# Two of 24 one-megabyte token loads are cut into three DMAs each

## The chip, the cores and the metric

The kernel runs on one core of a Trainium2 chip. The metric is the device time of one execution in microseconds (us). Before the change the median of three runs is 199.24 us (199.17 to 199.47).

## The reference: a gated recurrence, then a soft mixture of experts

Inputs are `x` and `f_logit`, both 4 batches x 5056 tokens x 256 channels in float32, a vector `lower_bound` of 256, and the weights `phi` (256 x 32), `w1` (8 x 256 x 1024) and `w2` (8 x 1024 x 256). The first stage is a recurrence over the tokens of each batch:

```
f = lower_bound + (1 - lower_bound) * sigmoid(f_logit)
h[t] = f[t] * h[t-1] + (1 - f[t]) * x[t]          # y[t] = h[t]
```

The second stage takes all 20224 rows of y as one list. `logits = y @ phi` gives 32 slots. A softmax over the rows weighs the rows into 32 slot inputs; each of the 8 experts takes four of them through `relu(slot @ w1) @ w2`; a softmax over the slots then mixes the 32 slot outputs back into every row. The output is 20224 x 256 in float32, 20.7 MB. The softmax over all rows means that no output row can be written before the whole recurrence and the experts are done.

## The kernel before: one ordered stream, then the experts, then the output

**Tiling.** The 5056 tokens of a batch are cut into 10 groups of 512 (the last but one is shorter). A unit `n` is one group of one batch, 40 in all. Units 8 to 31 are "long" ones: a pair of units (`n` even and `n + 1`) is 1024 consecutive tokens of one batch. `load(n)` brings a pair into an `f_t` tile and an `x_t` tile of 128 partitions x 2048 floats; partition p holds eight consecutive tokens, 8 KB that lie in one piece in memory. So a long pair is two DMAs of 1 MB (line 211), and there are 12 such pairs: n = 8, 10, ..., 30. The units before and after them are loaded with smaller DMAs (lines 225, 216 and 220). Each kind of tile has three buffers, so the load of pair n waits until the buffer of pair n - 6 has been read: `f_t` by ScalarE's sigmoid (line 235, `gate`), `x_t` by GpSimd's product (line 246, `enter`).

**The steps of a unit.** `gate`: ScalarE takes the sigmoid of a pair (`s_t`). `enter`: GpSimd multiplies it by x (`u_t`, one per unit). TensorE transposes both to channels (lines 261 and 267, `sp` and `up`). `decay`: ScalarE makes the factors `a` (lines 295, 302). `scan`: VectorE runs the recurrence along the tokens, two instructions per unit (line 313, `h`). TensorE transposes h back (line 326, `hp`), VectorE or ScalarE copies it out (line 343, `ht`); logits, exponentials and the accumulation of the slot inputs follow (lines 357, 366, 407).

**What sets the order.** The program is written out in order by hand (`manual_schedule`): each engine runs its instructions in the order of the loop over `n`, with waits on semaphores. All token loads are issued from the SP queue. `load(n + 6)` is called in iteration n, so the pair n = 20 is issued in iteration 14 and its sigmoid stands in iteration 16. The hardware DMAs issued from SP and ACT take their completion semaphores in turn from eight; a DMA waits for the DMA that used its semaphore before it.

**Weights.** The expert weights are loaded by the GpSimd queue (`load_w`, lines 136 and 146), cast from float32 to bf16 on the way, with the number per iteration in `W_AT`: 8 of w1, then 8 of w2, the last one in three parts. Most are issued after unit 31. The last two of w2 use an `f_t` buffer under the name `w_t`.

**The end.** After the last scan come the slot inputs, the two products of the experts (lines 624, 660, 671; line 671 is `so_ps` for experts 4 to 7, four groups of eight matmuls, the last sixteen of which read `w_t`), `slot_out` (lines 687, 688), and then the output stage: matmuls (708, 758), scaling by VectorE and ScalarE, and stores of up to 2 MB from SP (lines 734, 746, 772, 789). Short filler matmuls (`spin`, line 151, and `idle`, line 183) keep TensorE busy.

Of the kernel before, what the change touches and what calls it, by code (L numbers as in the profile page):

```python
# [18 lines left out]
def kernel(  # L19
# [10 lines left out]
    nc = tc.nc  # L30
# [5 lines left out]
    P = 128  # L36
    DC = D // P
    FC = F // P
    R = 4
    G = P * R  # L40
# [5 lines left out]
    def first(g):  # L46
        return g * G if g < n_grp - 1 else S - G
# [114 lines left out]
    with tc.tile_pool(name="sp2", bufs=3) as sp2, \  # L162
# [24 lines left out]
        def long(n):  # L187
            return 2 * B <= n < n_unit - 2 * B

        def place(n):  # L190
            if long(n):
                t, j = divmod(n, 2 * B)
                return 2 * t + j % 2, j // 2
            return divmod(n, B)
# [4 lines left out]
        def tokens(src, n, k):  # L199
            g, b = divmod(n, B)  # L200
            v = src[ds(b, k), ds(first(g), G)]
            return v.rearrange("b (p r) d -> p b r d", r=R)

        def load(n, k=2):
            for src, dst, tag in ((f_logit, fs, "f_t"), (x, xs, "x_t")):
                if n % 2 == 0:
                    dst[n // 2] = ld.tile([P, 2, R, D], F32, name=tag, tag=tag)
                t = dst[n // 2]
                if long(n):
                    g, b = place(n)  # L210
                    nc.sync.dma_start(
                        out=t.rearrange("p u r d -> p (u r) d"),
                        in_=src[b, ds(first(g), 2 * G)].rearrange("(p r) d -> p r d", r=2 * R))
                elif n // B == odd:
                    b, t0 = n % B, first(odd)
                    nc.sync.dma_start(
                        out=t[:, 0, R3],
                        in_=src[ds(b, 2), ds(t0 + P * R3, L)].rearrange("b t d -> t b d"))
                    for m in range(2):
                        nc.sync.dma_start(  # L220
                            out=t[:, m, ds(0, R3)],
                            in_=src[b + m, ds(t0, P * R3)].rearrange("(p r) d -> p r d", r=R3))
                else:
                    for m in range(n, n + k):
                        nc.sync.dma_start(out=t[:, ds(m % 2, 1)], in_=tokens(src, m, 1))
# [237 lines left out]
        for n in range(SINGLE):  # L463
            load(n, 1)
# [15 lines left out]
        for n in range(n_unit):  # L480
            if n < SINGLE - 2:
# [9 lines left out]
                if n % 2 == 0:  # L491
                    unit(load, n + AHEAD)
                unit(enter, n + 3)
                rep_constants(n)
            else:
                end = n >= n_unit - 6
                if n % 2 == 0:
                    unit(load, n + AHEAD)
                    if n == SINGLE - 2:
                        to_tokens(n - 1)  # L500
                        keep_tokens(n - 1)
                    if not end and n >= SETTLED:
                        unit(gate, n + 4)
                else:
                    unit(decay, n + 1)
                    if n < SETTLED:
                        gate(n + 3)
                    if n == n_unit - 5:
                        gate(n + 3)
                        exps(odd - 1)  # L510
# [37 lines left out]
                elif not end and long(n - 1):  # L548
                    if n % B == 0:
                        g = (n - 1) // (2 * B) * 2  # L550
# [48 lines left out]
    with tc.tile_pool(name="ew", bufs=1) as ew, \  # L599
# [35 lines left out]
        for q in range(E // Q):  # L635
# [4 lines left out]
            if q == 0:  # L640
                nc.tensor.matmul(cs_ps, rep2, cs1, start=True, stop=True)
                src = ht_ps.rearrange("p f (j s) -> p f j s", s=NS)[:, :, :, ds(0, SPE)]
                src = bass.AP(tensor=src.tensor, offset=src.offset,
                              ap=[list(src.ap[0]), [P, FC], [NS + SPE, Q], [1, SPE]])
# [6 lines left out]
            for j in range(Q):  # L651
                s0 = (Q + j) * SPE
                src = ht_ps[:, :, ds(j * NS + s0, SPE)]
# [177 lines left out]
```

## Time and profile before

| | |
|---|---|
| median of three runs | 199.24 us |
| the profiled execution's own time | 198.55 us |
| its span (first to last instruction) | 196.8 us |
| busy share of the span: PE, DVE, ACT, POOL | 77%, 73%, 70%, 52% |
| HBM read and written | 58.23 MB, 20.71 MB |
| 1 MB loads of `f_t`, of `x_t` | 12 and 12; 13.1 and 12.1 us from issue to landing (median) |
| the weights, `w_sb` of 512 KB written | 14 DMAs, 10.9 us from issue to landing (median) |

The profile shows one execution; times in it count from the start of the span. PE is TensorE, DVE VectorE, ACT ScalarE, POOL GpSimd, SP the engine that issues most DMAs. A row of a timeline is: start, duration, engine, line of the kernel, operation, written tile and read tiles, shape, number of instructions, and in brackets how long the engine stood idle before it and what ended that. The page cuts the span into 40 slices of 4.92 us; a digit is the busy share in tenths. A DMA runs on up to 16 DMA engines of the core; the trace keeps every packet with its start and duration, and for each DMA the moment at which each of its engines reported the end. A DMA has landed with the last of these.

### The profile page before, as it was taken

How to read it: one execution, taken by the hardware profiler on the slowest of the kernel's cores; microseconds unless marked ns; L12 is line 12 of the kernel's file. 1: busy time of each engine (PE TensorE's matmuls, PEld its weight loads, DVE VectorE, ACT ScalarE, POOL GpSimd, SP SyncE). 2: the span in 40 equal slices, each digit the busy share in tenths (PEclk: the TensorE clock that was granted, in tenths of full speed). 3: DMA queues.
4: the chain of work that ended last, by engine and by line, in shares of the span. 5: the costliest groups of instructions: out<-in, count | busy, mean ns of one | idle time of the engine just before them, and what ended most of it. 6: DMA issues, size and time to landing. Idle time of an engine off the chain costs nothing.

```text
span 196.8 us, 3233 instructions
## 1 busy us (share of the span) xinstructions
PE 151.1 (77%) x1198; PEld 105.9 (54%) x1198; DVE 143.4 (73%) x164; ACT 138.4 (70%) x195; POOL 103.2 (52%) x78
## 2 busy tenths in 40 slices
PE   0687589789979979997998878999979999950000
PEld 0475458577766857765776666558953533410000
DVE  2669789998899999999999999423278878740000
ACT  3688778899699998999997695622079799980000
POOL 2689586894988588894979967291030000000000
PEclk9999999996999999999999999999995555555555
DMA  5999999999999999999999999999739999999995
GB/s 203 418 423 417 430 430 420 428 426 338 403 425 428 393 343 423 426 413 306 406 422 376 265 221 213 213 213 214 130 136 424 428 444 433 426 430 426 426 426 216
DMA packets 14305, 70.75 MB, mean 360 GB/s; under 512 B 1601, under 2 KB 2882, under 8 KB 10322
## 3 DMA queue, kind: packets, MB, share of 16 engines
q1 hardware_dynamic: 11520, 62.00, 76.0%
q0 software_dynamic: 2624, 8.42, 21.5%
q8 instruction: 9, 0.15, 0.3%
q10 hardware_dynamic: 146, 0.13, 0.2%
q14 instruction: 6, 0.05, 0.1%
HBM read 58.23 MB, written 20.71 MB: 401 GB/s over the span
## 4 chain that ended last, share of the span: by engine, by line
PE 37%; DMA 22%; DVE 20%; issue 4%; POOL 4%; ACT 2%; ACTq 0%; SPq 0%; DVEq 0%; POOLq 0%
DVE h L313 15%; DMA x_t<-in_x_dram 14%; PE op L758 12%; DMA f_t<-in_f_logit_dram 7%; POOL u_t L246 4%; DVE ht L343 4%; PE hp L326 3%; PE up L267 3%; PE op L708 2%; PE so_ps L671 2%; PE sp L261 2%; PE lg L357 2%; PE slot_ps L407 1%; PE tail L151 1%; PE tail L390 1%
## 5 line engine op out<-in xcount | busy, mean ns | idle before, releaser
L246 POOL TENSOR_TENSOR u_t<-s_t,x_t 128x1024 bf16<-128x1024 bf16 (+1 forms) x39 | 82.5, 2127 | 22.4 <-ACT s_t L235 12.0
L313 DVE TENSOR_TENSOR_SCAN h<-a,h,up 128x512 bf16<-128x512 f32 (+1 forms) x72 | 86.9, 1252 | 3.7 <-PE up L267 2.5
L235 ACT ACTIVATE s_t<-f_t 128x2048 bf16<-128x2048 f32 (+2 forms) x23 | 38.4, 1669 | 7.2 <-DMA f_t<-in_f_logit_dram 7.2
L326 PE MATMUL hp<-ident_f,h 128*128 128x128 f32 (+1 forms) x160 | 29.2, 307 | 7.8 <-DVE ht L343 5.9
L326 PEld LDWEIGHTS hp<-ident_f,h 128*128 128x128 f32 (+1 forms) x160 | 23.4, 207 | 17.6 <-DVE ht L343 10.4
L261 PE MATMUL sp<-ident_f,s_t 128*128 128x128 f32 x144 | 21.3, 291 | 6.8 <-ACT s_t L235 4.6
L295 ACT ACTIVATE a<-sp,lbs 128x1024 f32<-128x1024 bf16 x24 | 25.4, 1115 | 0.6 <-PE sp L261 0.6
L758 PE MATMUL op<-slot_bd,etall 64*128 64x512 bf16 x62 | 24.5, 608 | 0.1
L769 ACT ACTIVATE oc<-op,rrow 128x256 f32<-128x256 f32 x60 | 22.7, 488 | 1.5 <-PE op L758 0.9
L763 DVE TENSOR_TENSOR oc<-op,rrow 128x1024 f32<-128x1024 f32 x16 | 19.3, 1222 | 4.7 <-PE op L758 4.5
L261 PEld LDWEIGHTS sp<-ident_f,s_t 128*128 128x128 f32 x144 | 17.3, 150 | 8.8 <-ACT s_t L235 5.1
L302 ACT ACTIVATE a<-sp,lbs 128x512 f32<-128x512 bf16 (+2 forms) x22 | 17.8, 856 | 3.8 <-PE sp L261 3.5
L267 PE MATMUL up<-ident_f,u_t 64*128 64x64 f32 x192 | 17.6, 230 | 2.4 <-POOL u_t L246 2.4
L183 PE MATMUL slot_ps<-rep,ident_f 128*128 128x256 f32 x54 | 17.7, 423 | 1.0 <-POOL rep L86 1.0
L267 PEld LDWEIGHTS up<-ident_f,u_t 64*128 64x128 f32 x192 | 13.9, 138 | 6.3 <-POOL u_t L246 2.8
L758 PEld LDWEIGHTS <-etall 64*128 64x128 bf16 x62 | 9.1, 154 | 14.1 <-issue 11.4
L343 DVE COPY ht<-hp 128x512 f32<-128x512 f32 (+1 forms) x22 | 14.7, 670 | 1.4 <-PE hp L326 1.4
L343 ACT COPY ht<-hp 128x512 f32<-128x512 f32 (+1 forms) x18 | 10.4, 580 | 6.6 <-PE hp L326 6.5
L313 DVE TENSOR_TENSOR_SCAN h<-a,up 128x512 bf16<-128x512 f32 x8 | 9.3, 1208 | 2.5 <-PE up L261 2.5
L183 PEld LDWEIGHTS slot_ps<-rep,ident_f 128*128 128x128 f32 x54 | 8.6, 194 | 3.4 <-issue 1.3
L357 PE MATMUL lg<-h,phi 128*32 128x512 bf16 (+1 forms) x80 | 9.6, 390 | 0.0
L261 PE MATMUL up<-ident_f,u_t 128*128 128x128 f32 x48 | 8.9, 312 | 0.5 <-POOL u_t L246 0.5
(108 smaller groups left out, 146.5 us busy)
## 6 DMA issues: line engine op xcount, KB each, us to landing
f_t<-in_f_logit_dram SPq DMA_DIRECT2D x12, 1024.0 KB, 13.1
x_t<-in_x_dram SPq DMA_DIRECT2D x12, 1024.0 KB, 12.1
out_dram<-oc SPq DMA_DIRECT2D x6, 2048.0 KB, 11.8
w_sb<-in_moe_w_dram POOLq DMA_DIRECT2D x14, 512.0 KB, 10.9
f_t<-in_f_logit_dram SPq DMA_DIRECT2D x12, 512.0 KB, 8.4
x_t<-in_x_dram SPq DMA_DIRECT2D x12, 512.0 KB, 9.9
out_dram<-oc SPq DMA_DIRECT2D x4, 896.0 KB, 5.8
out_dram<-ob SPq DMA_DIRECT2D x1, 2048.0 KB, 9.0
```

The lines of the kernel that those rows point to most:

```text
L183: nc.tensor.matmul(slot_bank[:, 1], ident_f, wide_rep, start=False, stop=False, skip_group_check=True)
L235: nc.scalar.activation(s_t, f_t, ACT.Sigmoid, scale=-1.0)
L246: nc.gpsimd.tensor_tensor(uts[n][:, :r], s_t[:, :r], x_t[:, :r], ALU.mult)
L261: nc.tensor.transpose(ps[:, :, r], t[:, r], ident_f)
L267: nc.tensor.transpose(v[:, :, r], t(r)[k].bitcast(F32), ident_f[k, k])
L295: nc.scalar.activation(a, sp[:, :, :, :, o], ACT.Identity, scale=nomlb[:, ds(o, 1)], bias=1.0)
L313: nc.vector.tensor_tensor_scan(h[:, :T, o], decays[n // 2, o][:, n % 2, :T], up[:, :T, o], hs[number(g - 1, b)][:, ds(used(g - 1) - 1, 1), ...
L326: nc.tensor.transpose(hp[:n_p, r], hw[:, :n_p, r], ident_f)
L343: copy(hts[g][:n_p, b].rearrange("p r d -> p (r d)").bitcast(F32), hps.pop(n)[:n_p].rearrange("p r c -> p (r c)"))
L758: nc.tensor.matmul(op[:, i_r].rearrange("p u d -> p (u d)"), ew[:, :, r + i_r], slot_bd[ds(j * 2 * NS, 2 * NS)].rearrange("s u d -> s (u d)"),
L763: nc.vector.tensor_tensor(ob[:, :, ds(r, k)].rearrange("p u r d -> p r u d"), op[:, ds(0, k)], scale[:, ds(r, k)].unsqueeze(3).broadcast_t ...
L769: nc.scalar.activation(ob[:, u, r + i_r], op[:, i_r, u], ACT.Copy, scale=scale[:, r + i_r, ds(u, 1)])
```

## The change: n = 20 is loaded as 112 + 8 + 8 partitions

For the pair n = 20 each of the two 1 MB loads (`f_t` and `x_t`) becomes three DMAs into the same tile: partitions 0 to 111, 112 to 119 and 120 to 127. The other 22 long loads stay one DMA of 128 partitions. The bytes, their places and the order of the loads are the same; SP issues four DMAs more.

```diff
+        SKEWED = 20
+
         def load(n, k=2):
...
                 if long(n):
                     g, b = place(n)
-                    nc.sync.dma_start(
-                        out=t.rearrange("p u r d -> p (u r) d"),
-                        in_=src[b, ds(first(g), 2 * G)].rearrange("(p r) d -> p r d", r=2 * R))
+                    into = t.rearrange("p u r d -> p (u r) d")
+                    rows_in = src[b, ds(first(g), 2 * G)].rearrange("(p r) d -> p r d", r=2 * R)
+                    shares = (P - 16, 8, 8) if n == SKEWED else (P,)
+                    for i, k in enumerate(shares):
+                        part = ds(sum(shares[:i]), k)
+                        nc.sync.dma_start(out=into[part], in_=rows_in[part])
```

## The prediction

> **What bounds the kernel now.** I read the page's slices first, then the chain of work that ended last, then the rows around the three places where a load can hold the end: the sigmoid of pair 20, the recurrence on VectorE, and the last weights.
>
> ```profile
> DMA   5999999999999999999999999999739999999995
> GB/s 203 418 423 417 430 430 420 428 426 338 403 425 428 393 343 423 426 413 306 406 422 376 265 221 213 213 213 214 130 136 424 428 444 433 426 430 426 426 426 216
> ```
>
> The sixteen DMA engines are full from slice 1 to slice 27 (5 to 138 us) and again in the output stage. The 213 GB/s of slices 23 to 27 is no idleness: the weights are read as float32 and written as bf16, so the engines still read some 426 GB/s. One stream of loads and weights thus runs without a gap until about 142 us.
>
> ```profile
> 39.50 14.40 DMA f_t<-in_f_logit_dram
> 60.78 2.35 DVE h L313 x2
> 140.74 1.88 PE so_ps L671 x16
> 142.64 0.36 DVE slot_out L687
> 155.50 19.24 PE op L758 x48
> ```
>
> The chain goes over loads until 53.90 us (pair 18's `f_t`), then over VectorE and TensorE. At the end of the middle part it stands on the last sixteen products of the experts, then `slot_out`, then the output stage, whose 2 MB stores leave at the full DMA rate (slices 30 to 38) and end the span. So whatever moves `slot_out` moves the end by as much. Those sixteen products against the eight before them:
>
> ```profile
> 137.59 1.03 PE L671 MATMUL so_ps<-w_sb,wide 128*128 128x256 bf16 x8
> 140.57 2.03 PE L671 MATMUL so_ps<-w_t,wide 128*128 128x256 bf16 x16
> 127.62 0.53 POOL L146 DMA_DIRECT2D w_t<-in_moe_w_dram  x1 [1.91 <-DMA w_sb<-in_moe_w_dram]
> DMA to landing us min/median/max: 14.6/17.3/18.5
> 140.00:142.00 2.00, 2.00 (x21) 1.78 (x20) 0.76 (x2) 0.00 (x0) 0.00 (x0) 1.00 0.59 96
> ```
>
> One takes 0.273 us by its own row, and eight take 1.03, so they follow each other at (1.03 - 0.273) / 7 = 0.108 us. Sixteen should take 0.273 + 15 x 0.108 = 1.89 and took 2.03: about 0.13 us of waiting. The last `w_t` part is issued at 127.62 and, with the shortest time to landing of the four, lands at 142.2, where the wait ends. Landing and TensorE are level there: the landing ends last, by 0.13 us.
>
> The last row is the table by stage (PE, PEld, DVE, ACT, POOL, then the granted clock 1.00, the DMA share 0.59 and GB/s). In 140 to 142 us the engines are only 59% busy: some are through long before others. The trace's landing marks say how unequal. Against the earliest engine, the sixteen end the last weight DMA at 0, .14, .20, .38, .52, .85, .86, .91, 1.28, 1.36, 1.42, 1.50, 1.64, 1.66, 1.70 and 1.86 us. For the first loads the spread is 0.4 us. The steps come with the fetches of instructions (queue q8, 16 KB packets) and ACT tables (q14, 8 KB), each served by one engine: the one at 29.4 us sets one engine back 1.4 us behind its fellows, and it stays back, since no engine ever runs out of work to catch up in.
>
> **The change part by part.**
>
> *The split of the bytes.* A 1 MB load is 128 rows of 8 KB, eight to an engine. At 16 engines and 428 GB/s (slices 4 and 5 have 430) a row takes 8192 / 26.75 = 0.306 us on its engine; the packet records have the same step. 112 rows give seven to each engine. The 8-row pieces are the question: no row before shows one. From one side there is `lb_row`, one row. Queue q10 holds it and one output store of 128 rows, 146 packets in all: 128 + 16 completions for the store leave one packet and one completion for it, so one row used one engine. From the other side, a load of 128 rows uses all sixteen. I take eight engines with a row each, nearest to one engine for a row. If both pieces use the same eight, those get 7 + 1 + 1 = 9 rows and the other eight get 7. Over `f_t` and `x_t` that is +2 rows and -2 rows: the first eight end everything later by 2 x 0.306 = 0.61 us, the others earlier by 0.61. The bounds: pieces spread over sixteen shift nothing; a piece on a single engine puts 7 + 16 rows there against 8, 15 more, twice, 30 x 0.306 = 9.2 us.
>
> [...]
>
> *The shift at the end.* The engines are never idle, so a shift at 60 us is still there at 142. The last landing becomes the larger of (latest of the loaded eight + 0.61) and (latest of the others - 0.61). Which of the sixteen the loaded eight are, no view tells. If the engine at 1.86 is among them, +0.61. If the latest among them is the one at 1.70, 1.66 or 1.64, then +0.45, +0.41 or +0.39. Half the chance lies on the first, most of the rest on the next two: I take +0.5. The end waits on this landing already, so the price is paid in full.
>
> *Pair 20 in mid stream.* The same shift reaches the loads: `f_t` of pair 20 by up to 0.31 us, all later ones by up to 0.61.
>
> ```profile
> 58.94 1.91 ACT L235 ACTIVATE s_t<-f_t 128x2048 bf16<-128x2048 f32 x1 [0.24 <-DMA f_t<-in_f_logit_dram]
> 61.68 0.75 PE L326 MATMUL hp<-ident_f,h 128*128 128x128 f32 x4
> 61.78 2.15 POOL L246 TENSOR_TENSOR u_t<-s_t,x_t 128x1024 bf16<-128x1024 bf16 x1 [0.94 <-PE lg L357]
> 63.73 2.45 DVE L313 TENSOR_TENSOR_SCAN h<-a,h,up 128x512 bf16<-128x512 f32 x2
> 70.28 5.01 DVE L313 TENSOR_TENSOR_SCAN h<-a,h,up 128x512 bf16<-128x512 f32 x4
> ```
>
> ScalarE's sigmoid waits for this load. Behind it on ScalarE stand the copy `ht` (60.76, ends 61.33) and the decays, and TensorE's `hp` at 61.68 waits for `ht`: 0.3 us late is just covered by the 0.35 between. GpSimd's product starts at 61.78, and x lands by the marks at 61.25; 0.61 late is 61.86, 0.1 us lost. The scan that needs these products starts at 70.28, 2 us after its transposes. VectorE is the bound here and its row shows next to no idle time; from pair 24 on, the `f_t` and `x_t` waits of ScalarE and GpSimd (0.5 to 0.6 us each) grow by 0.6 under about 1 us of room before the next scan. Zero, with at most 0.3 us on the way to a place where the landing of the weights is late by more.
>
> *Four more DMAs on SP.* Each issue takes 0.33 us, and two follow the first at 47.16 and at 51.56. The eight semaphores now come round sooner: the `f_t` of pair 22, issued at 51.98, must wait for pair 18's (landed 53.90), 1.9 us later; that of pair 24 (56.31) for pair 20's first piece, about 2.5 us later. Behind them SP has only more loads. By the landing marks their data start at about 59.6 and 64.6 us, when the queue gets to them, so 5 us or more remain. Cost 0 as long as the queue holds over 2 MB; without that cover 2 us.
>
> *Fixed cost of a small DMA.* In the packet records one load follows another on an engine with a completion packet of some 6 ns between: four more on eight engines, 0.02 us. The other bound is the small token DMAs of line 216 (128 KB), which by the marks end 0.3 to 1.0 us before the next: at most 4 us if a 64 KB piece cost that alone. I take 0.02, the row of the same queue in the same state. [...]
>
> *Sum.* 0.5 + 0 + 0 + 0.02 = +0.5 us on the profiled execution's 198.55 (span 196.8 and 1.75 around it), 199.05. That execution is 0.69 below the median of the runs; on 199.24 the forecast is 199.75 us. What a measurement of this kernel can tell from no change is about 0.2%, 0.40 us.
>
> **The rivals.**
>
> *A, the forecast: a late engine gets the extra rows.* For it: eight engines lie at 1.28 or later, and it takes only one of the four latest among the loaded eight. 199.6 to 199.9. Chance 0.64.
>
> *B, not slower: the late ones are all relieved.* If the four latest are all among the relieved eight and no loaded engine was beyond 1.25 us, the last weight lands earlier. For it: exactly eight engines lie beyond 1.25, as if they were one half. If so, the landing moves to the larger of 1.86 - 0.61 and .91 + 0.61, 0.34 us earlier, but TensorE then ends last, and only the 0.13 us of waiting is gained: 199.1. More could come only through the waits on loads in mid stream, which VectorE covers. Chance 0.20, of which 0.07 beyond the measurement.
>
> *C, no shift:* the pieces go over all sixteen, or each over a different eight. 199.24. Against it: `lb_row`. Chance 0.10.
>
> *D, the pieces are dear:* one engine takes a whole piece, or each pays on its own. 203 to 208. Chance 0.06.
>
> **How the numbers follow.** Of A four fifths lie beyond 0.40 us (the cases at 0.61, 0.45 and 0.41): 0.51; D adds 0.06, C's scatter 0.01: slower 0.58. Faster is B's 0.07 and 0.02 of C's scatter: 0.09. The same: 0.33. The range takes A with 0.1 us of scatter, and B and C below: 199.0 to 200.0; it leaves out D and B's larger gain. A's own range is 199.6 to 199.9.
>
> **What would show it.** In the profile after: pair 20's pieces with 8 completions each; engines of the last `w_t` DMA ending up to 0.6 us later against TensorE's sixteen products, which then take 2.4 to 2.6 us in place of 2.03; `slot_out` at about 143.1; VectorE's scans as before. If `w_t` lands by 142.0 and the sixteen take 1.9, B holds. The forecast fails if a gap in the engines' work lets the late ones catch up, or if the fetches fall on other engines in other executions.

## The result: 2.9% slower, and the profile after

The changed kernel takes 204.63 us in the median (204.09 to 205.72, four runs) against 199.36 us (199.17 to 199.88) for the kernel before on the same chip: 1.0288 times as long, 95% interval 1.0248 to 1.0327. The forecast of 199.75 us (199.0 to 200.0) was wrong by 4.9 us. Here and below, medians and ranges are over all executions of a kernel, while ratios leave out those that took over 1.5% longer than its fastest. The profiled execution took 205.11 us with a span of 203.3 (before 198.55 and 196.8).

The rows of the page that answer to those shown of before are the DMA digits and the GB/s of its 40 slices, now 5.08 us each:

```profile
DMA  6999999999999999999999999999929999999996
GB/s 210 420 417 422 430 429 422 429 421 336 384 201 201 372 375 372 417 432 386 322 417 420 297 253 211 215 211 214 194 66 361 400 426 432 442 416 451 422 416 258
```

The digits are 9 as before. The rate under them is not: slices 11 and 12 (56 to 66 us) have 201 GB/s where the kernel before had 425 or more. No cast explains it, as it does for the weights in slices 23 to 27 (211 to 253 GB/s; their queue moves 8.42 MB by the page, half of their 16.8 MB in float32); these are token loads. The slices before them have the old rate, and from slice 16 on it is back. The same stretch by time, first the changed kernel, then the one before; the last three columns are the granted clock, the DMA share and GB/s:

```profile
53.00:55.00 2.00, 2.00 (x19) 1.81 (x18) 1.61 (x2) 1.46 (x2) 2.00 (x2) 1.00 1.00 422
55.00:58.40 3.40, 3.40 (x31) 2.89 (x29) 3.32 (x4) 3.40 (x4) 2.96 (x2) 1.00 1.06 258
58.40:60.60 2.20, 1.44 (x11) 1.09 (x10) 2.20 (x4) 0.13 (x1) 2.20 (x2) 1.00 1.06 160
60.60:64.00 3.40, 2.19 (x21) 1.19 (x19) 3.40 (x4) 1.43 (x1) 1.14 (x1) 1.00 0.99 227
64.00:66.80 2.80, 1.79 (x14) 1.58 (x15) 1.26 (x3) 2.80 (x4) 0.00 (x0) 0.98 1.01 161
```

```profile
55.00:58.40 3.40, 2.39 (x18) 1.75 (x17) 3.30 (x5) 3.40 (x4) 2.70 (x2) 1.00 1.01 424
58.40:60.60 2.20, 2.20 (x22) 2.01 (x20) 2.20 (x2) 1.96 (x2) 2.20 (x2) 1.00 1.00 425
60.60:64.00 3.40, 3.23 (x26) 1.87 (x24) 3.31 (x5) 3.38 (x5) 2.46 (x3) 1.00 1.01 429
64.00:66.80 2.80, 2.69 (x28) 2.30 (x28) 2.80 (x4) 2.77 (x4) 2.61 (x2) 1.00 1.01 413
```

The pieces pass in the order of the queue: the 112 rows of `f_t` at 258 GB/s, its two pieces of 8 at 160, the 112 of `x_t` at 227, its pieces of 8 at 161. Against the rates before, the four stretches lose 3.4 x (1 - 258/424) + 2.2 x (1 - 160/425) + 3.4 x (1 - 227/429) + 2.8 x (1 - 161/413) = 1.33 + 1.37 + 1.60 + 1.71 = 6.0 us. The packet records say how: the median 8 KB packet has 309 ns in every microsecond of this stretch before; here it is 0.56 us while a 112 piece passes and 0.96 to 0.99 us with the pieces of 8. It is not one engine: from 56 to 58 us every one of the packets that start takes 0.46 us or more. The DMA share stays at 0.99 to 1.06, since a packet that is held up still counts as busy.

In mid stream the forecast's "zero" has become these rows of the timeline of the changed kernel:

```profile
59.38 4.89 DVE L318 TENSOR_TENSOR_SCAN h<-a,h,up 128x512 bf16<-128x512 f32 x4
62.57 1.91 ACT L240 ACTIVATE s_t<-f_t 128x2048 bf16<-128x2048 f32 x1 [4.04 <-DMA f_t<-in_f_logit_dram]
65.01 0.75 PE L331 MATMUL hp<-ident_f,h 128*128 128x128 f32 x4 [2.22 <-ACT ht L348]
66.50 2.46 DVE L318 TENSOR_TENSOR_SCAN h<-a,h,up 128x512 bf16<-128x512 f32 x2
68.41 2.15 POOL L251 TENSOR_TENSOR u_t<-s_t,x_t 128x1024 bf16<-128x1024 bf16 x1 [6.67 <-DMA x_t<-in_x_dram]
```

ScalarE waits 4.04 us for `f_t` where it waited 0.24, GpSimd 6.67 us for `x_t`, and VectorE, busy throughout 64.0 to 66.8 us before (2.80 of 2.80 in the window above), is busy for 1.26 of it: its scans stop at 64.27 and go on at 66.50. The end of the chain, with what moved the end of the whole run:

```profile
134.07 14.58 DMA w_t<-in_moe_w_dram
148.64 0.04 issue
148.69 0.39 PE so_ps L676 x2
149.08 0.03 issue
149.10 0.36 DVE slot_out L692
```

The last weights land at 148.64 us instead of 142.18, 6.46 later, `slot_out` starts 6.46 later (149.10 for 142.64), and the execution is 205.11 - 198.55 = 6.56 longer. In this execution what the stream loses at 60 us is paid in full at the end, as the forecast had it; only the loss was another.

### The profile page after: what moved, and what is told of

Read it like the earlier page. It is cut to its first block, busy times and chain, and to the rows that moved or that the text cites. A ratio compares the mean times of both kernels' runs of the same rounds, so it can differ in the third digit from the quotient of the medians.

```text
span 203.3 us, 3241 instructions
## 1 busy us (share of the span) xinstructions
PE 157.3 (77%) x1198; PEld 110.4 (54%) x1198; DVE 143.5 (71%) x164; ACT 138.3 (68%) x195; POOL 103.1 (51%) x78
## 3 DMA queue, kind: packets, MB, share of 16 engines
q0 software_dynamic: 2624, 8.42, 20.8%
## 4 chain that ended last, share of the span: by engine, by line
DMA 32%; PE 27%; DVE 9%; POOL 8%; issue 6%; ACT 6%; SPq 2%; ACTq 0%; POOLq 0%
PE op L763 11%; DMA x_t<-in_x_dram 11%; DMA w_sb<-in_moe_w_dram 8%; DMA w_t<-in_moe_w_dram 7%; DVE h L318 7%; DMA f_t<-in_f_logit_dram 6%; POOL u_t L251 6%; PE hp L331 3%; PE up L272 3%; PE op L713 2%; PE sp L266 2%; PE slot_ps L183 2%; SPq L230 1%; ACT oc L774 1%; DVE ht L348 1%
## 5 line engine op out<-in xcount | busy, mean ns | idle before, releaser
L331 PE MATMUL hp<-ident_f,h 128*128 128x128 f32 (+1 forms) x160 | 30.3, 316 | 8.7 <-DVE ht L348 5.1
L331 PEld LDWEIGHTS hp<-ident_f,h 128*128 128x128 f32 (+1 forms) x160 | 24.4, 209 | 18.6 <-DVE ht L348 9.3
L266 PE MATMUL sp<-ident_f,s_t 128*128 128x128 f32 x144 | 23.6, 312 | 6.6 <-ACT s_t L240 4.5
L763 PE MATMUL op<-slot_bd,etall 64*128 64x512 bf16 x62 | 25.0, 623 | 0.2 <-ACT oc L774 0.2
L266 PEld LDWEIGHTS sp<-ident_f,s_t 128*128 128x128 f32 x144 | 19.4, 163 | 8.5 <-ACT s_t L240 5.0
L183 PE MATMUL slot_ps<-rep,ident_f 128*128 128x256 f32 x54 | 18.9, 447 | 0.0
L183 PEld LDWEIGHTS slot_ps<-rep,ident_f 128*128 128x128 f32 x54 | 9.1, 204 | 2.5 <-issue 1.5
L266 PE MATMUL up<-ident_f,u_t 128*128 128x128 f32 x48 | 9.5, 330 | 0.5 <-POOL u_t L251 0.5
```

The costliest lines, as they stand in the source:

```text
L183: nc.tensor.matmul(slot_bank[:, 1], ident_f, wide_rep, start=False, stop=False, skip_group_check=True)
L266: nc.tensor.transpose(ps[:, :, r], t[:, r], ident_f)
L331: nc.tensor.transpose(hp[:n_p, r], hw[:, :n_p, r], ident_f)
L763: nc.tensor.matmul(op[:, i_r].rearrange("p u d -> p (u d)"), ew[:, :, r + i_r], slot_bd[ds(j * 2 * NS, 2 * NS)].rearrange("s u d -> s (u d)"),
```

## The experiments

In the tables "landing" is that of the last weights in the profiled execution of the run (142.18 in the kernel before); it tells best what the stream lost, since the time of one kernel scatters by a microsecond and more from execution to execution.

The landing is not always what sets the time, for a second path leads to `slot_out`: the recurrence, then the experts' products on TensorE. In all fourteen profiled executions `slot_out` starts at the later of two moments, 0.46 us after the landing or 17.94 us after the end of the last scan. In the kernel before these are 142.64 and 142.52 (the last scan ends at 124.58), in the change 149.10 and 148.35 (130.41). In eight of the twelve experiments the recurrence is the later one: three DMAs of 128 partitions, 112 + 16, 64 + 64, the spread rows, both runs with `f_t` alone, and both runs with four added DMAs. Much of the scatter comes in on this path before pair 20 is loaded, at 20 to 33 us. First the kernel before, then the one with spread rows (below), which does the same work there:

```profile
20.00:33.00 13.00, 9.30 (x71) 7.42 (x71) 11.21 (x12) 10.44 (x10) 9.75 (x7) 1.00 1.02 428
```

```profile
20.00:33.00 13.00, 9.91 (x57) 7.58 (x58) 9.17 (x10) 8.19 (x8) 9.71 (x7) 0.74 1.02 427
```

With a granted clock of 0.74 in this window (0.5 for 6.8 of the 13 us) VectorE does two instructions fewer, and the scan that starts at 31.81 us before starts 2.13 us later. So it was in all fourteen: the ten executions with a clock of 0.74 or 0.87 here were 0.7 to 2.3 us late at that scan, and the four with 1.00 by at most 0.04.

The theories:

- *The late engine*: the forecast. Rows are shared out unevenly, nothing is slower in itself.
- *Fixed price*: each DMA costs on its own, the second half of rival D.
- *The pieces of 8*: they alone are dear, since half of the engines work on them (eight landing marks in place of sixteen when their data land).
- *The partitions*: a DMA is slow because of the partitions that its engines write at the same time.
- *The addresses read*: the same, for the addresses in memory that it reads.

### Three DMAs, but of all 128 partitions

```diff
-                    shares = (P - 16, 8, 8) if n == SKEWED else (P,)
+                    shares = (4, 2, 2) if n == SKEWED else (2 * R,)
...
-                        nc.sync.dma_start(out=into[part], in_=rows_in[part])
+                        nc.sync.dma_start(out=into[:, part], in_=rows_in[:, part])
```

> Both loads of pair 20 are cut into three DMAs along the row: all 128 partitions each time, 4, 2 and 2 KB of each 8 KB row. Number of DMAs, order, buffers and waits are those of the change. Theory 'each DMA has a fixed price': 204.6 us, as with the change. Theory 'the partitions': a DMA that spans less than 128 partitions is slow in itself, so here nothing is lost: 199.4 us (the kernel before in the same comparison as the change had 199.36), at most 0.5 more. Theory 'the late engine' of the prediction: 199.4 too.

Measured: 199.18 us against 199.16, ratio 1.0016 (0.999 to 1.0041); landing 142.16. The stretch of pair 20:

```profile
55.00:59.00 4.00, 3.57 (x28) 2.43 (x26) 3.91 (x4) 3.71 (x5) 4.00 (x3) 1.00 1.03 407
60.00:64.00 4.00, 4.00 (x37) 2.82 (x35) 4.00 (x5) 3.98 (x5) 3.18 (x3) 1.00 1.02 426
```

Same number of DMAs, same order, same waits on semaphores, and nothing is lost, though the packets are of 4 and 2 KB. The fixed price falls, and with it everything that SP's queue or the semaphores could have done.

### 112 + 16

```diff
-                    shares = (P - 16, 8, 8) if n == SKEWED else (P,)
+                    shares = (P - 16, 16) if n == SKEWED else (P,)
```

> Pair 20 is cut into 112 and 16 partitions, two DMAs per load, both on sixteen engines. Theory 'the pieces of 8 are dear, since only half the engines work on them': 199.4 us. Theory 'fixed price': one added DMA instead of two, 199.36 + 5.27 / 2 = 202.0 us. Theory 'the partitions': the packets of the 112 piece took about 0.55 us in the profile of the change, so 2 x 7 x (0.55 - 0.306) = 3.4 us stay lost even if the 16 rows go at full rate, 202.8 us; if these collide as well, up to 204.6.

Measured: 203.52 us (203.3 to 203.94), ratio 1.0227 (1.0188 to 1.0267); landing 146.76, +4.58. The loss is nearly that of the change, so the pieces of 8 are not needed for it. In the change a piece of 112 rows has sixteen landing marks; if sixteen engines share these two pieces, 112 and 16 rows are seven and one for each, and by this count the uneven shares are not needed either.

### 64 + 64, and 64 in the middle

```diff
-                    shares = (P - 16, 8, 8) if n == SKEWED else (P,)
+                    shares = (64, 64) if n == SKEWED else (P,)
```

> Pair 20 is cut into partitions 0 to 63 and 64 to 127, two DMAs per load, four rows on each engine from each. Theory 'fixed price': 202.0 us, as 112 + 16. Theory 'pieces of 8': 199.4. Theory 'the partitions': slow, with packets of about 0.6 us through both pieces. [...]

```diff
-                    shares = (P - 16, 8, 8) if n == SKEWED else (P,)
-                    for i, k in enumerate(shares):
-                        part = ds(sum(shares[:i]), k)
+                    shares = ((32, 64), (0, 32), (96, 32)) if n == SKEWED else ((0, P),)
+                    for at, k in shares:
+                        part = ds(at, k)
```

> Pair 20 is cut into partitions 32 to 95, 0 to 31 and 96 to 127, three DMAs per load. Theory 'fixed price': three DMAs as in the change, 204.6 us. Theory 'fewer partitions, less rate, wherever they lie': as 64 + 64 or slower, 204 to 205. Theory 'which partitions are written at the same time': the 64 in the middle go at the full rate (packets of 0.31 us) and only the two pieces of 32 are slow; with 0.61 us a row these lose 4 x 0.306 = 1.22 us per load, 2.45 in all: 201.8 us. [...]

Measured: 64 + 64 takes 205.36 us (204.12 to 206.98), ratio 1.0322 (1.0256 to 1.0388), landing 148.51. With 32 to 95 first it is 203.83 us (202.64 to 203.9), ratio 1.0227 (1.018 to 1.0273), landing 147.32. The two first pieces are the same DMA but for the start: 64 rows of 8 KB. The stretch in which they pass, first partitions 0 to 63, then partitions 32 to 95 and the pieces behind:

```profile
54.90:56.10 1.20, 1.20 (x16) 1.03 (x13) 1.20 (x2) 1.20 (x2) 1.20 (x1) 1.00 1.17 177
```

```profile
54.90:56.10 1.20, 0.97 (x8) 0.50 (x6) 1.11 (x2) 1.20 (x2) 1.20 (x1) 1.00 1.08 430
56.30:58.30 2.00, 1.64 (x14) 1.42 (x14) 2.00 (x4) 2.00 (x3) 1.62 (x2) 1.00 1.06 180
```

177 against 430 GB/s, packets of 0.8 to 1.0 us (from 55 to 56 us) against 0.309: "fewer partitions, less rate" falls, and where the 64 lie decides. The sixteen engines are busy in both windows (DMA share 1.17 and 1.08). Two later windows of the 64 + 64 run have 172 (56.3 to 58.3 us) and 240 GB/s (62.5 to 64). The size was not as expected: with 32 to 95 first 4.5 us are lost instead of 2.45, and the slow packets of 64 + 64 take 0.8 to 1.0 us instead of about 0.6. The 0.61 us a row of the expected 2.45, twice 0.306, was the author's estimate, and no run shows it: 180 GB/s in the second window above are 8192 / (180 / 16) = 0.73 us a row on each of sixteen engines. The second load's middle piece does not reach the full rate either (its packets take 0.5 us at 60 us); whether the slow pieces ahead of it are the cause, and by how much it and they contribute, no run separates.

### The same partitions, other addresses

```diff
-                    shares = (P - 16, 8, 8) if n == SKEWED else (P,)
+                    shares = ((32, 0, 64), (0, 64, 32), (96, 96, 32)) if n == SKEWED else ((0, 0, P),)
...
+                    for to, at, k in shares:
+                        nc.sync.dma_start(out=into[ds(to, k)], in_=rows_in[ds(at, k)])
```

> As the cut into 32 to 95, 0 to 31 and 96 to 127, but the first 64 rows of memory go into partitions 32 to 95 and rows 64 to 95 into partitions 0 to 31 (the tokens of pair 20 thus stand in another order, which the output shows). Theory 'the written partitions decide': the first piece of the first load runs at 0.31 us a packet as in that run, and the time is its 203.8 us. Theory 'the addresses read decide': the first piece reads what partitions 0 to 63 of the 64 + 64 cut read, whose packets took 0.8 to 1.0 us, so it is slow from the start.

Measured: 203.56 us (202.0 to 204.8), ratio 1.0218 (1.0164 to 1.0272); landing 145.85. The first piece reads exactly the rows that partitions 0 to 63 got at 177 GB/s, and writes 32 to 95:

```profile
54.90:56.10 1.20, 0.90 (x7) 0.42 (x5) 1.11 (x2) 1.20 (x2) 0.88 (x1) 1.00 0.96 403
56.30:58.30 2.00, 1.64 (x13) 1.43 (x14) 2.00 (x4) 2.00 (x3) 1.70 (x1) 1.00 1.05 213
```

403 GB/s, and from 55 to 56 us no packet of it takes over 0.309 us. The addresses read fall; for these 64 rows the written partitions decide.

### Eight rows, spread or side by side

Two added DMAs of 8 rows of 4 KB behind each whole load of pair 20, into a weight buffer that is loaded later, at partitions j, j + 4, ..., j + 28; the second kernel has `ds(8 * j, 8)`, eight side by side, and is otherwise the same:

```diff
+        spare = w2_sb[5].rearrange("p f d -> p (f d)").bitcast(F32).rearrange("p (r d) -> p r d", d=D)
...
+                    nc.sync.dma_start(out=into, in_=rows_in)
+                    if n == SKEWED:
+                        for i in range(2):
+                            j = i + 2 * (tag == "x_t")
+                            part = ds(j, 8, 4)
+                            nc.sync.dma_start(out=spare[part], in_=rows_in[part, :R])
```

> Pair 20 is loaded as before, one DMA of 128 partitions per load; behind each stand two added DMAs of 8 rows of 4 KB into a weight buffer that is not in use yet, at partitions j, j + 4, ..., j + 28 (32 x 4 KB = 128 KB more are read). No work is left out. Theory 'the late engine' (the forecast's own step): eight engines get 4 x 0.153 = 0.61 us more, the end moves by 0 (the latest engine is not among them) to 0.61, 199.2 + 0.5 = 199.7 us. [...] Theory 'a DMA of 8 rows is dear whatever it writes': 4 x (0.48 - 0.153) = 1.3 us more (half of the 0.96 us that such packets of 8 KB took in the changed kernel), 201 us.

> The same four added DMAs, but each to eight neighbouring partitions (0 to 7, 8 to 15, 16 to 23, 24 to 31). Theory 'the late engine': as the spread ones, 199.7 us. Theory 'the written partitions': packets of 4 KB at about 0.48 us or more, 4 x (0.48 - 0.153) = 1.3 us more than the spread ones: 201.0 us, and up to 202 if the loads behind them are slowed as well.

Measured: spread 199.87 us (198.82 to 201.26, 12 runs), ratio 1.0043 (1.0013 to 1.0073), landing 142.53. Side by side 199.7 us (199.28 to 201.17), ratio 1.0025 (0.9996 to 1.0054), landing 143.45. The windows in which the added pieces pass, first spread, then side by side:

```profile
57.00:58.00 1.00, 1.00 (x11) 0.89 (x10) 0.92 (x2) 1.00 (x3) 1.00 (x2) 1.00 1.09 455
60.00:61.00 1.00, 0.47 (x4) 0.48 (x5) 1.00 (x2) 0.89 (x1) 1.00 (x1) 1.00 1.04 438
```

```profile
57.00:58.00 1.00, 1.00 (x13) 0.88 (x11) 1.00 (x2) 1.00 (x2) 1.00 (x2) 1.00 1.10 356
60.00:61.00 1.00, 1.00 (x11) 0.92 (x9) 1.00 (x2) 1.00 (x1) 1.00 (x1) 1.00 1.12 324
```

Spread, eight rows move the landing as the forecast's step says: by 0.35 us (expected 0 to 0.61), with the engines' ends 2.19 us apart instead of 1.86. The time of 199.87 us (0.26 to 1.45 us longer, 199.7 expected) doesn't confirm it, since in the profiled execution the end stands on the recurrence. TensorE's last sixteen products start behind the landing of 142.53 and take 1.76 us, without a wait:

```profile
142.66 1.76 PE so_ps L679 x16
144.44 0.36 DVE slot_out L695
```

The landing alone would have allowed 142.99. The recurrence is 2.13 us late at 32 us, before any of the added pieces moved, and 1.92 at its end, so the time is no proof of the step, and its agreement with 199.7 is luck as far as the trace tells. Side by side the rate of the whole stream dips, and the landing is another 0.92 us later (expected 1.3). There the end stands on the landing (`slot_out` at 143.91), and the profiled execution takes 199.28 us against 200.3 with the spread rows. So the times of these two kernels can't settle the 0.92; 201.0 was expected side by side. The four added pieces support the theory of the partitions by their windows and landings, not by the time. The rows that they read differ too (four apart or neighbours), which this pair alone doesn't separate.

### One cut load, and where its price lies

```diff
-                    shares = (P - 16, 8, 8) if n == SKEWED else (P,)
+                    shares = (P - 16, 8, 8) if n == SKEWED and tag == "f_t" else (P,)
```

> The change at the f_t load of pair 20 alone (112, 8 and 8); x_t as before. Theory 'the stream loses at each cut load what its packets lose': half of the change's loss, 199.2 + 2.6 = 201.8 us. Theory 'the loss comes once, from a stall of the stream': 204.6 us as with both. Theory 'the x_t load is what hurts, f_t is covered': 199.4 us.

> The f_t load alone cut into 112, 8 and 8, once more with more rounds, since its four runs lay between 201.0 and 204.8 us. Theory 'each cut load costs what its packets lose' (its profiled execution: last weights 2.8 us later than in the kernel before): 201.0 to 202.0 us. Theory 'one cut load costs nearly as much as two': 203.5 us again.

> The x_t load alone cut into 112, 8 and 8. Theory 'each cut load costs what its packets lose': half of the change's 5.3 us, 201.0 to 202.2 us. Theory 'one costs nearly as much as two': 203.5 us. Theory 'f_t is what hurts': 199.4.

| cut | time, us | ratio, 95% interval | landing |
|---|---|---|---|
| `f_t` | 203.69 (201.0 to 204.84) | 1.0184 (1.0117 to 1.025) | 144.94 |
| `f_t`, again | 203.02 (201.29 to 203.91) | 1.019 (1.0151 to 1.023) | 145.39 |
| `x_t` | 202.03 (201.34 to 203.09) | 1.0155 (1.0123 to 1.0186) | 145.42 |
| both (the change) | 204.63 (204.09 to 205.72) | 1.0288 (1.0248 to 1.0327) | 148.64 |

By the landings each load pays its own share: +2.8 and +3.2 for `f_t`, +3.2 for `x_t`, 6.0 to 6.4 together, and the change has +6.46. By the times the two single cuts cost 3.8 and 3.1 us (0.019 and 0.0155 of 198.76), 6.9 together, more than the 5.7 of both, and most runs with `f_t` alone lie 0.8 to 2.9 us above the execution that was profiled (201.0 and 201.94 us). So for `f_t` the loss lies between "half" (at most 2.8 us) and "nearly as much as two" (4.3); for `x_t` "half" came about (202.03 us in 201.0 to 202.2). That neither load is covered by other work is shown. The two kernels' times aren't quite like with like: in both profiled executions with `f_t` alone the recurrence was 2.1 and 2.3 us late at 32 us, with a granted clock of 0.74, and it set the end, 0.1 and 0.2 us later than the landing alone would have; with `x_t` alone the clock was 1.00 and the landing set it. What the recurrence did in the executions without a profile is open, and so is their excess.

### 112 partitions without any piece of 8

Two added DMAs behind each whole load of pair 20, into four weight buffers that are loaded later; the yardstick has `P` in place of `P - 16`:

```diff
+                    nc.sync.dma_start(out=into, in_=rows_in)
+                    if n == SKEWED:
+                        for i in range(2):
+                            spare = spares[i + 2 * (tag == "x_t")]
+                            nc.sync.dma_start(out=spare[:P - 16], in_=rows_in[:P - 16, ds(R * i, R)])
```

> All loads whole as before; behind each load of pair 20 two added DMAs of 128 partitions x 4 KB into weight buffers not in use yet (2 MB more are read in all). No work is left out. At 0.153 us per 4 KB and eight of them per engine and DMA, 4 x 8 x 0.153 = 4.9 us more, 204.1 us. It is the yardstick for the next run.

> The same four added DMAs with 112 partitions each, nothing in pieces of 8. At full rate they take 7/8 of 4.9, 4.3 us: 203.5 us, less than with 128 partitions (theory 'only the pieces of 8 are slow', and theory 'the late engine'). Theory 'the partitions': the packets of the 112 piece took 0.55 us for 8 KB in the changed kernel, so 4 x 7 x 0.275 = 7.7 us: 206.9 us, 2.8 us more than with 128 partitions although fewer bytes are moved.

Measured: 203.81 us with 128 partitions, ratio 1.0246 (1.0214 to 1.0279), landing 147.05; 208.36 us (206.28 to 209.75) with 112, ratio 1.0392 (1.0347 to 1.0437), landing 150.38. The windows in which the two pairs pass, first 128, then 112:

```profile
57.00:60.00 3.00, 3.00 (x27) 2.60 (x26) 2.69 (x4) 2.76 (x3) 3.00 (x2) 1.00 1.03 422
62.50:66.00 3.50, 3.33 (x31) 2.62 (x29) 3.50 (x5) 3.12 (x4) 1.81 (x1) 1.00 1.04 426
```

```profile
57.00:60.00 3.00, 2.32 (x19) 1.73 (x19) 3.00 (x4) 1.81 (x3) 3.00 (x3) 1.00 1.03 310
62.50:66.00 3.50, 3.33 (x27) 2.53 (x24) 3.50 (x5) 3.47 (x4) 0.00 (x0) 1.00 1.00 310
```

An eighth less to move, and 2.9 us longer by the ratios (0.0146 of 198.76; 3.3 by the landings; 2.8 were expected). 112 partitions are slow with nothing beside them but whole loads. That they are slow because of where their engines write follows from the test with 64 rows, not from one with 112: seven rows to an engine instead of eight is a rival that no run separates.

## Why the prediction was wrong, point by point

- **The split of the bytes** is the step that failed. It held where it counted engines: by the landing marks a piece of 8 has one mark within 0.5 us of the issue and eight when its data land, where a load of 128 or 112 has sixteen. That all the pieces of 8 use the same eight engines, on which the 0.61 us of the sum rests, no run shows; with eight rows spread the landing moved by 0.35 us. It failed where it priced them: "a row takes 8192 / 26.75 = 0.306 us on its engine" was read from loads of 128 partitions, and was carried over to other partition ranges as a property of the engine. In a 112 piece a row takes about 0.56 us, and 0.96 with the pieces of 8. The step's bound of 9.2 us stood on engines with too many rows, and the range left it out with rival D. Before, only a few single packets took 0.56 us or more; the doubt would have been in order because every long load there had all 128 partitions.
- **The shift at the end** held for the landing: with eight rows added at partitions four apart it moved by 0.35 us. In the change the engines' ends lie 2.49 us apart for 1.86, which is of the same size; beside 6.46 us it doesn't matter. The steps by which engines fell behind come with packets of q8 and q14, which the page calls "instruction" alike; that those of q14 bring ACT tables was the author's naming. "The price is paid in full" held in the change, where the landing ended last by 0.75 us. It was read from one execution, in which the granted clock was 1.00 from 20 to 33 us and the landing ended last by 0.12; where the recurrence ends last, as by 0.43 us with three DMAs of 128 partitions, such a shift is covered.
- **Pair 20 in mid stream**: the order of the work was read rightly and the lateness was wrong, so the cover was used up. The last piece of `f_t` landed at 62.46 (issued at 49.27, with 13.19 us on the chain of waits) instead of 58.84, 3.6 us late against a cover of 0.35. The recurrence ends 5.83 us later than before, which alone would have put `slot_out` at 148.35 in place of 149.10; the landing is later still.
- **Four more DMAs on SP** and the **fixed cost of a small DMA** held, both as zero: three DMAs of 128 partitions cost nothing (199.18 us against 199.16).
- **The rivals.** D had the size (203 to 208 us) and neither of its two causes: the pieces were on eight engines by their marks, and three DMAs cost no more than one (199.18 us against 199.16). The pieces of 8 were dear for another reason, and the two windows with a 112 piece lost as much (2.9 us of the 6.0). A missing rival was "the pieces move at another rate". B and C didn't come about.

What stays open is the size. At 0.306 us a row, seven rows would take 7 x 0.306 = 2.14 us. The trace has 3.4 us and more for a piece of 112, and every packet that starts from 56 to 58 us takes 0.46 us or more. Whether an engine that is held up holds up others, and by what path, no run here shows.

## What to carry to other kernels

In a stream that bounds the kernel, cut a load along the row and keep all 128 partitions in every DMA: that cost nothing here (199.18 us against 199.16), while a cut along the partitions into 112, 8 and 8 cost 2.8 to 3.2 us more (by the landings) for a megabyte that takes 2.45 whole. A price per row or per byte stands for the partition range from which it was read (0.306 us a row with 128 partitions, 0.56 in a 112 piece), and a change of that range needs a rival of its own. Read the GB/s beside the busy share: 161 GB/s stood at a DMA share of 1.01, since an engine whose packets are slow counts as busy. And before a time is taken as proof of a term, look which path ended last in that execution.

## What the runs showed of the hardware

- The rate of these loads of 64 rows went with the partitions that they write: 177 GB/s for 0 to 63 and 430 for 32 to 95, with as many rows and the sixteen engines busy in both windows (DMA share 1.17 and 1.08), and 403 for 32 to 95 from the addresses that had 177 with 0 to 63.
- Two pieces of 32 KB, each written to eight neighbouring partitions, lower the whole stream: 356 and 324 GB/s in the two windows of 1 us, against 455 and 438 with the rows four partitions apart.
- Ten executions had a granted clock of 0.74 or 0.87 from 20 to 33 us, and their recurrence was 0.7 to 2.3 us late at 32 us; the four with 1.00 were late by at most 0.04.
- Packets stay slow for a short time behind the slow pieces. In the change the packets of the whole loads behind pair 20 still have a median of 0.356 us between 67 and 68 us, and 0.309 from 68 us on.
